# Attention, Fourier mixing and feed-forward in one kernel: the folded third token chunk contracted over all 128 rows in place of 97, 33 and 96

## The chip, the core and the metric

The kernel runs on one core of a Trainium2 chip. The metric is the device time of one execution in microseconds (us). Five engines work beside each other: TensorE (PE in the profile, with its weight loads as PEld), VectorE (DVE), ScalarE (ACT), GpSimd (POOL) and SyncE (SP, which issues the DMAs here). Before the change, three runs gave a median of 1114.37 us (1114.26 to 1114.49).

## The reference

Inputs are q, k, v of shape (8, 8, 576, 64), that is 8 batches, 8 heads, 576 tokens and 64 channels per head, and two weight matrices of 512 x 2048 and 2048 x 512.

```python
# attention, window of 128 tokens, with a slope of its own for each head
scores = scale * q @ k.T ; scores + bias inside the window, -1e9 outside
attn = softmax(scores) ; x = attn @ v          # heads side by side: (8, 576, 512)
# mixing
u = x + real(fft(fft(x, axis=tokens), axis=channels))
un = (u - mean) / sqrt(var + 1e-6)
out = u + relu(un @ w_ch1) @ w_ch2
```

The change lies in the Fourier step over the tokens.

## The kernel before, in words

**The whole.** The 8 batches are worked through in a pipeline. While one batch is in attention, the batch before it is in the Fourier step and the one before that in the feed-forward network. Each piece of work is a small Python function that is put in a queue with a due time (`put`, `after`); the queue is emptied in order of due time while the program is built, and this sets the order of the instructions on each engine. Nothing reorders the matmuls later: TensorE takes them as they come, so Fourier matmuls stand between score matmuls (`scores`, L382), value matmuls (`values`, L444 to L451) and the feed-forward matmuls (`ffn`, L720 and L734).

**Precision.** Most products are made of float16 halves: a number is the sum of a high and a low float16, and a product is high by high, low by high and high by low, added up in PSUM. In batches 0 and 1 the attention runs in float32.

**The Fourier step of a batch** is the function `fourier`. The 576 tokens are folded by symmetry (token t with token 576 - t), so that 289 token frequencies are computed from 289 folded tokens, in three chunks of 128, 128 and 33 (the array `X` and its third tile `X2`). The channels are folded too, into four groups `g` of 128 channels: groups 0 and 1 need the cosine table, groups 2 and 3 the sine table.

- `fold_a` to `fold_d` (L508 to L566) make the folded chunks. Chunks 0 and 1 give a high tile `fh` and a low tile `fl` of 128 rows each. The third chunk has only 33 rows for the cosine and 32 for the sine. Its halves are stacked in one tile of 128 partitions, called `stack` (and `stack1` for one extra channel): for the cosine groups the high half in rows 0 to 32 and the low half in rows 64 to 96; for the sine groups the high half in rows 0 to 31 and again in rows 32 to 63, the low half in rows 64 to 95. `stack` and `stack1` are set to zero once at the start (L122, L123).
- `rows(g)` (L568) multiplies: for each group, six matmuls of 128 rows for chunks 0 and 1, and then the third chunk. For the cosine groups that is one matmul over the first 97 rows of `stack` (high by high and low by high at once) and one over its first 33 rows (high by low); for the sine groups one over 96 rows does all three. Each matmul moves 289 columns of the table `tab1_sb` past 128 stationary columns and has a line of the profile, L576. The result goes through `rows_hi` on ScalarE (L580) and `rows_lo` on VectorE (L584) into float16 halves.
- `middle` (L586, matmuls at L593) does the same for one extra channel. Here the table is stationary and the moving operand is one column. It runs over three parts `j` of the frequencies (128, 128 and 33 wide), each with six matmuls of 128 rows, one of 97 and one of 33.
- `cols` (L604, matmuls at L610) is the Fourier step over the channels, `cols_out` and `cols_add` bring it back into `X`, and `norm` prepares the feed-forward input `uT`, which a transposing DMA writes.

In the third chunk of the table, `tables` sets everything to zero and then fills in (L826 to L828): entry 0 holds the cosine's high half in rows 0 to 32 and again in rows 64 to 96, entry 1 its low half in rows 0 to 32, entry 2 the sine's high, low and high halves in rows 0 to 31, 32 to 63 and 64 to 95.

Of the kernel before, what the change touches and what calls it, by code (L numbers as in the profile page):

```python
# [55 lines left out]
def begin_of(p):  # L56
    return 6 * PACE[0] * p if p < 4 else T1 + 6 * (p - 4)
# [6 lines left out]
def forward_of(b):  # L64
    return transform_of(b) + (START - DFT if b else 11 * PACE[1])
# [11 lines left out]
def attn_fft_ffn_kernel(  # L77
# [31 lines left out]
    tab1_sb = const.tile([128, 4, 3, NS], F16, name="tab1_sb")  # L109
# [11 lines left out]
    stack1 = const.tile([128, 1], F16, name="stack1")  # L121
# [369 lines left out]
    def bank(b):  # L491
        if b == 0:
            p = next(spare)
            return p.tile([128, 512], F32, name="fp" if p is ps_f else "pd")
        return ps_d.tile([128, 512], F32, name="pd")

    def fourier(b, t0):
# [70 lines left out]
        def rows(g):  # L568
            zp = st["zp", g] = bank(b)
            o = 0 if g < 2 else 2  # L570
            prods = [(st["in", c][l][:, g], tab1_sb[:, o + t, c]) for c in range(2) for l, t in ((0, 0), (1, 0), (0, 1))]
            rest = stack[:, 128 * g:128 * g + 128]
            for t, m in ((0, 97), (1, 33)) if g < 2 else ((2, 96), ):
                prods.append((rest[:m], tab1_sb[:m, t, 2]))
            for x, (l, r) in enumerate(prods):
                T.matmul(zp[:, :NS], l, r, start=(x == 0), stop=(x == len(prods) - 1))  # L576

# [8 lines left out]
        def middle():  # L586
            gps = st["gps"] = bank(b)
            for j, (j0, mj) in enumerate(SCH):
                prods = [(tab1_sb[:, t, c, j0:j0 + mj], st["in", c][2][:, x:x + 1])
                         for c in range(2) for t, x in ((0, 0), (0, 1), (1, 0))]  # L590
                prods += [(tab1_sb[:m, t, 2, j0:j0 + mj], stack1[:m]) for t, m in ((0, 97), (1, 33))]
                for x, (l, r) in enumerate(prods):
                    T.matmul(gps[:mj, j:j + 1], l, r, start=(x == 0), stop=(x == len(prods) - 1))  # L593

# [54 lines left out]
        t = t0 + f * 2.6  # L649
        for g in range(4):  # L650
            put(t, rows, g)
            put(t + f * 0.3, rows_hi, g)
            put(t + f * 0.5, rows_lo, g)
            t += f * 0.75
        put(t, middle)
        put(t + f * 0.2, middle_out)
        t += f * 0.55
# [86 lines left out]
    for p in range(4 * B):  # L744
        b, j = divmod(p, 4)
        t, f = begin_of(p), 1 if b else PACE[0]
# [23 lines left out]
    for b in range(B):  # L770
        t = begin_of(4 * b)
# [4 lines left out]
        t = forward_of(b)  # L776
# [119 lines left out]
```

## Time and profile before

| | before |
|---|---|
| median of 3 runs | 1114.37 us |
| time of the profiled execution | 1109.96 us |
| its span | 1108.2 us |
| around the span | 1.8 us |
| TensorE busy (matmuls) | 1061.6 us, 96% of the span |
| TensorE weight loads busy | 740.5 us, 67% |
| VectorE busy | 722.2 us, 65% |
| ScalarE busy | 584.8 us, 53% |
| mean granted TensorE clock | 0.961 |
| Fourier matmuls with the third chunk, L576 | 48 (16 of 97 rows, 16 of 33, 16 of 96) |
| the same, L593 | 48 (24 of 97 rows, 24 of 33) |

Matmuls overlap, and a matmul's duration in the profile is from its start to its modelled end. What a matmul costs TensorE is read from the start of one to the start of the next. In a row of the timeline the first number is the start in us from the span's start, the second the time that the row's instructions cover, then come engine, line, operation, out<-in, the array part that a matmul takes (rows*columns), the moving operand (rows x columns, type) and the number of instructions (x). An idle time before it and what ended it stand in brackets. The profiled execution's time is 4.4 us below the median of the runs; differences are taken between executions of one kind.

### The profile page before, as it was taken

How to read it: one execution, taken by the hardware profiler on the slowest of the kernel's cores; microseconds unless marked ns; L12 is line 12 of the kernel's file. 1: busy time of each engine (PE TensorE's matmuls, PEld its weight loads, DVE VectorE, ACT ScalarE, POOL GpSimd, SP SyncE). 2: the span in 40 equal slices, each digit the busy share in tenths (PEclk: the TensorE clock that was granted, in tenths of full speed). 3: DMA queues.
4: the chain of work that ended last, by engine and by line, in shares of the span. 5: the costliest groups of instructions: out<-in, count | busy, mean ns of one | idle time of the engine just before them, and what ended most of it. 6: DMA issues, size and time to landing. Idle time of an engine off the chain costs nothing.

```text
span 1108.2 us, 23754 instructions
## 1 busy us (share of the span) xinstructions
PE 1061.6 (96%) x9188; PEld 740.5 (67%) x9188; DVE 722.2 (65%) x2105; ACT 584.8 (53%) x1388; POOL 21.4 (2%) x61
## 2 busy tenths in 40 slices
PE   6989979989797999999999999999999999999998
PEld 5777767565564767667667677585857577767665
DVE  6989378837884576787868485969685755362111
ACT  5867589757855655456635464456535441241000
POOL 0000000000100000000000000001000000010000
PEclk9989569999899999999999999999999999999999
DMA  9951246667765544343643145334532240020000
GB/s 368 313 194 57 59 131 179 175 169 178 160 169 164 139 102 105 75 98 68 139 84 80 41 106 104 86 82 102 121 77 48 49 90 1 20 54 14 20 10 20
DMA packets 191506, 117.81 MB, mean 106 GB/s; under 512 B 154400, under 2 KB 164128, under 8 KB 191392
## 3 DMA queue, kind: packets, MB, share of 16 engines
q1 hardware_dynamic: 190816, 114.84, 40.6%
q8 instruction: 72, 1.18, 0.4%
q10 hardware_dynamic: 576, 1.45, 0.3%
q14 instruction: 42, 0.34, 0.1%
HBM read 70.63 MB, written 9.44 MB: 72 GB/s over the span
## 4 chain that ended last, share of the span: by engine, by line
PE 78%; DVE 8%; DMA 7%; ACT 4%; issue 2%; SPq 0%; POOL 0%; ACTq 0%; DVEq 0%
PE fp L720 31%; PE fp L734 27%; PE sp L382 6%; PE pv L444 3%; PE pd L576 3%; DMA wall<-q_dram 2%; DMA wall<-v_dram 2%; PE fp L303 2%; PE sp L425 1%; PE pd L610 1%; DMA uT<-un 1%; ACT wall L261 1%; DMA pt<-P 1%; PE pv L449 1%; DVE P L394 1%
## 5 line engine op out<-in xcount | busy, mean ns | idle before, releaser
L734 PE MATMUL fp<-wall,hbuf 128*128 128x512 f16 x1728 | 392.1, 379 | 0.3 <-DVE hbuf L162 0.3
L720 PEld LDWEIGHTS <-wall 128*128 128x128 f16 x3840 | 339.6, 99 | 63.6 <-issue 15.2
L720 PE MATMUL fp<-uT,wall 128*128 128x256 f16 x3072 | 366.1, 276 | 15.8 <-DVE hbuf L162 9.5
L734 PEld LDWEIGHTS <-hbuf 128*128 128x128 f16 x1728 | 161.8, 98 | 182.2 <-issue 3.5
L162 ACT ACTIVATE P<-P,nb 128x256 f32<-128x256 f32 x320 | 142.0, 479 | 107.1 <-DVE nb L394 107.0
L725 ACT ACTIVATE hbuf<-fp 128x512 f16<-128x512 f32 x144 | 84.9, 590 | 186.6 <-PE fp L720 186.6
L162 DVE SCALAR_TENSOR_TENSOR hbuf<-fp,hbuf 128x512 f16<-128x512 f32 x144 | 98.8, 687 | 127.5 <-ACT hbuf L725 127.1
L394 DVE CUSTOM_DVE_ANT_0 P<-sp,rg,nsl 128x256 f32<-128x256 f32 x240 | 97.5, 450 | 53.1 <-PE sp L382 48.5
L162 DVE SCALAR_TENSOR_TENSOR P<-P 128x256 f16<-128x256 f32 x240 | 88.7, 390 | 23.4 <-ACT P L407 21.9
L382 PE MATMUL sp<-kk,qq 64*128 64x256 f16 (+5 forms) x880 | 97.1, 297 | 6.5 <-DMA kk<-k_dram 5.3
L407 ACT ACTIVATE P<-P 128x256 f16<-128x256 f32 x240 | 85.2, 383 | 2.0 <-DMA pt<-P 1.7
L261 ACT ACTIVATE wall<-wall 128x512 f32<-128x512 f32 (+2 forms) x90 | 54.6, 607 | 50.2 <-DMA wall<-v_dram 23.2
L449 PE MATMUL pv<-vhs,pt 128*128 128x65 f16 x432 | 55.9, 196 | 4.6 <-DVE nmr L687 4.3
L450 PE MATMUL pv<-vl,pt 128*128 128x64 f16 x432 | 56.5, 194 | 0.0
L451 PE MATMUL pv<-vhs,pt 128*128 128x65 f16 x432 | 56.4, 195 | 0.0
L162 DVE SCALAR_TENSOR_TENSOR X<-fp,misc,X 128x512 f32<-128x512 f32 x32 | 23.8, 745 | 43.6 <-PE fp L734 43.6
L444 PE MATMUL pv<-vr,pt 128*128 128x65 f32 x288 | 47.7, 326 | 4.0 <-issue 2.3
L449 PEld LDWEIGHTS <-pt 128*128 128x128 f16 x432 | 41.3, 98 | 14.7 <-issue 7.7
L444 PEld LDWEIGHTS pv<-vr,pt 128*128 128x128 f32 x288 | 45.1, 242 | 7.6 <-issue 4.9
L382 PEld LDWEIGHTS <-qq 64*128 64x128 f16 (+1 forms) x720 | 31.3, 99 | 24.4 <-issue 20.6
L720 PE MATMUL fp<-wall,wall 128*128 128x128 f16 x768 | 45.4, 219 | 0.1
L450 PEld LDWEIGHTS <-pt 128*128 128x128 f16 x432 | 41.0, 99 | 6.4
(159 smaller groups left out, 1201.8 us busy)
## 6 DMA issues: line engine op xcount, KB each, us to landing
qr<-q_dram SPq DMA_DIRECT2D x32, 304.0 KB, 3.1
hbuf<-w_dram SPq DMA_DIRECT2D x16, 512.0 KB, 6.7
out_dram<-X SPq DMA_DIRECT2D x32, 256.0 KB, 2.4
wall<-v_dram SPq DMA_DIRECT2D x30, 256.0 KB, 2.9
vr<-v_dram SPq DMA_DIRECT2D x24, 320.0 KB, 3.4
kr<-k_dram SPq DMA_DIRECT2D x24, 289.0 KB, 3.3
wall<-q_dram SPq DMA_DIRECT2D x24, 256.0 KB, 2.9
wall<-k_dram SPq DMA_DIRECT2D x24, 256.0 KB, 2.8
```

Source lines behind the costliest of these rows:

```text
L162: put(now[0] + dt, lambda: f(*a, **kw))
L261: A.activation(t, t, AF.Square, accum_out=box["mx"][:, i, c:c + 1])
L382: T.matmul(sp[e][:m, col:col + n], qq[h, c0:c0 + m], keys(kk[h], ti), start=(x == 0), stop=(x == len(prods) - 1))
L394: V.tensor_tensor_reduce(pt[:m, 0:n], sp[e][:m, col:col + n], tab[:m, pc:pc + n], mul, 3.0e38, ALU.add, ALU.min, nb[:m, ti:ti + 1])
L407: A.activation(hi, P32, AF.Copy, scale=2.0 ** 14)
L444: T.matmul(pv[:, ti], pt[:, col:col + 128], ops[p][2][:, e, vc], start=first, stop=last)
L449: T.matmul(pv[:, ti], ph, vh[:, e, vc], start=first, stop=False)
L450: T.matmul(pv[:, ti, 0:D], ph, vl[:, e, vc], start=False, stop=False)
L451: T.matmul(pv[:, ti], pl, vh[:, e, vc], start=False, stop=last)
L720: T.matmul(fp[:, i * n:(i + 1) * n], w1_ap(e, c, f0 + i), uT[:, j, c, 0:n], start=(c == 0 and p == 0), stop=(c == 3 and p == 2))
L725: A.activation(ht[:, 0], fp, AF.Relu)
L734: T.matmul(op, hh[f][:, a, i * 128:(i + 1) * 128], w2_ap(e, f), start=(f == 0 and p == 0), stop=(f == 15 and p == 2))
```

## The change

The slices are dropped. `rows` and `middle` multiply over all 128 rows of `stack` and `stack1` and of the third chunk of the table. Between and behind the halves either the stacked tile or the table is zero (or both), so the sums stay the same. No instruction is added or removed, and the order of the instructions on all five engines, their waits included, is the same row by row in the built programs.

```diff
@@ rows(g)
             rest = stack[:, 128 * g:128 * g + 128]
-            for t, m in ((0, 97), (1, 33)) if g < 2 else ((2, 96), ):
-                prods.append((rest[:m], tab1_sb[:m, t, 2]))
+            for t in (0, 1) if g < 2 else (2, ):
+                prods.append((rest, tab1_sb[:, t, 2]))
             for x, (l, r) in enumerate(prods):
                 T.matmul(zp[:, :NS], l, r, start=(x == 0), stop=(x == len(prods) - 1))
@@ middle()
                 prods = [(tab1_sb[:, t, c, j0:j0 + mj], st["in", c][2][:, x:x + 1])
                          for c in range(2) for t, x in ((0, 0), (0, 1), (1, 0))]
-                prods += [(tab1_sb[:m, t, 2, j0:j0 + mj], stack1[:m]) for t, m in ((0, 97), (1, 33))]
+                prods += [(tab1_sb[:, t, 2, j0:j0 + mj], stack1) for t in (0, 1)]
                 for x, (l, r) in enumerate(prods):
                     T.matmul(gps[:mj, j:j + 1], l, r, start=(x == 0), stop=(x == len(prods) - 1))
```

## The prediction

> **What bounds the kernel now.** I read the page first (busy times and the chain of waits), then the table of stages, then TensorE's waits, and last the timeline around the Fourier matmuls.
>
> ```profile
> span 1108.2 us, 23754 instructions
> PE 1061.6 (96%) x9188; PEld 740.5 (67%) x9188; DVE 722.2 (65%) x2105; ACT 584.8 (53%) x1388; POOL 21.4 (2%) x61
> PE 78%; DVE 8%; DMA 7%; ACT 4%; issue 2%; SPq 0%; POOL 0%; ACTq 0%; DVEq 0%
> ```
>
> TensorE carries 78% of the chain that ends last. The rest must be placed in time, since time saved on TensorE ahead of a wait for another engine may be lost there. The table of stages has, after the stretch, busy us of PE, PEld, DVE, ACT and POOL, then the granted clock and the DMA share:
>
> ```profile
> 104.00:144.00 40.00, 39.30 (x192) 29.14 (x191) 19.25 (x59) 22.58 (x58) 0.17 (x2) 0.53 0.22 64
> 144.00:170.00 26.00, 19.91 (x110) 15.93 (x107) 20.50 (x67) 22.67 (x57) 1.70 (x6) 0.68 0.58 145
> 355.00:362.00 7.00, 3.03 (x16) 2.14 (x16) 3.05 (x7) 5.92 (x17) 0.00 (x0) 0.51 0.52 140
> 385.00:968.00 583.00, 581.38 (x5510) 398.22 (x5509) 409.54 (x1201) 288.88 (x688) 11.24 (x27) 1.00 0.36 80
> ```
>
> From 385 to 968 us TensorE is busy for 581.38 of 583 us at full clock: nothing else sets the pace there, and five of the eight Fourier steps (batches 3 to 7) lie in it. Before 385 us there are gaps, and stretches at about half clock. TensorE's waits (in all, times, longest) put names to them:
>
> ```profile
> PE fp L720 <- DVE hbuf L162: 9.5, 6, 6.6
> PE pv L449 <- DVE nmr L687: 4.3, 1, 4.3
> ```
>
> **The change part by part.** No instruction is added, removed or moved, and none waits for anything new. What can change is only the time of each matmul over the third chunk. First, a cosine group of batch 4 in the timeline, then a sine group of the same batch:
>
> ```profile
> 602.79 0.30 PE L576 MATMUL pd<-tab_sb,fh 128*128 128x289 f16 x1
> ...
> 603.42 0.29 PE L576 MATMUL pd<-tab_sb,fh 128*128 128x289 f16 x1
> 603.54 0.51 PE L576 MATMUL pd<-tab_sb,stack 97*128 97x289 f16 x2
> 603.99 2.69 PE L720 MATMUL fp<-uT,wall 128*128 128x256 f16 x23
> ```
>
> ```profile
> 616.14 0.29 PE L576 MATMUL pd<-tab_sb,fh 128*128 128x289 f16 x1
> 616.26 0.29 PE L576 MATMUL pd<-tab_sb,stack 96*128 96x289 f16 x1
> 616.39 1.58 PE L720 MATMUL fp<-uT,wall 128*128 128x256 f16 x13
> ```
>
> From start to start a matmul of 128 rows takes 603.54 - 603.42 = 0.12 us; the six from 602.79 to 603.54 take 0.75, or 0.125 each. The one of 96 rows takes 616.39 - 616.26 = 0.13, the same. But the pair of 97 and 33 rows takes 603.99 - 603.54 = 0.45, where two plain ones take 0.25. So 0.20 us is lost around the 33 rows, and none around 96 or 97. I read it as two stops of the array of about 0.10 us, one going into the 33 rows and one coming out. Whatever the mechanism, a product of 128 rows with neighbours of 128 rows is what the first six are, so I price the changed pair at 0.25 us. The sine groups change from 0.13 to 0.125: nothing.
>
> A cosine group gains 0.20 us and there are two in a batch: **0.40 us per batch**.
>
> [...]
>
> Now the middle step of the same batch:
>
> ```profile
> 621.96 0.29 PE L593 MATMUL pd<-a,tab_sb 128*128 128x1 f16 x6
> 622.11 0.27 PE L593 MATMUL pd<-stack,tab_sb 97*128 97x1 f16 x2
> 622.32 0.30 PE L593 MATMUL pd<-a,tab_sb 128*128 128x1 f16 x6
> 622.48 0.27 PE L593 MATMUL pd<-stack,tab_sb 97*128 97x1 f16 x2
> 622.68 0.30 PE L593 MATMUL pd<-a,tab_sb 128*33 128x1 f16 x6
> 622.85 0.27 PE L593 MATMUL pd<-stack,tab_sb 97*33 97x1 f16 x2
> 623.05 1.47 PE L734 MATMUL fp<-wall,hbuf 128*128 128x512 f16 x6
> ```
>
> Six matmuls with one column take 0.15 us (621.96 to 622.11), or 0.025 each, so a pair would take 0.05. The three pairs take 0.21, 0.20 and 0.20: 0.15 too much each, in two stops of some 0.075. That is six stops in the step. But the third part is only 33 columns wide, and other matmuls of that width show that this is a stop too:
>
> ```profile
> 519.32 0.38 PE L734 MATMUL fp<-wall,hbuf 128*128 128x512 f16 x1
> 519.63 0.23 PE L610 MATMUL pd<-tab_sb,zh 128*33 128x129 f16 x1
> 520.26 0.22 PE L610 MATMUL pd<-tab_sb,zh 128*33 128x127 f16 x1
> 520.41 0.82 PE L734 MATMUL fp<-wall,hbuf 128*128 128x512 f16 x3
> ```
>
> These two rows of 33 columns are the first and the last of twelve. The last takes 520.41 - 520.26 = 0.15 us up to the full-width matmul, where the eleven before it take (520.26 - 519.63) / 11 = 0.06 each: again a stop of about 0.09. So after the change two of the six stops stay, one into the narrow part and one out of it. Four go, worth 4 x 0.075 = **0.30 us per batch**. If the narrow part stopped nothing, all six would go (0.45); if the four stops left behind half their price, 0.15. I take 0.30.
>
> In batch 0 the clock is at half, and a stop there may cost more:
>
> ```profile
> 121.64 0.80 PE L576 MATMUL fp<-tab_sb,stack 97*128 97x289 f16 x2
> 122.38 0.42 PE L576 MATMUL pd<-tab_sb,fl 128*128 128x289 f16 x1
> 122.59 0.45 PE L576 MATMUL pd<-tab_sb,fh 128*128 128x289 f16 x1
> 122.83 0.80 PE L576 MATMUL pd<-tab_sb,stack 97*128 97x289 f16 x2
> 123.57 0.42 PE L576 MATMUL fp<-tab_sb,fl 128*128 128x289 f16 x1
> ```
>
> The pairs take 0.74 each, two plain ones 2 x 0.24 (122.59 to 122.83): 0.26 lost, 0.52 for both groups, with the middle step about 0.8 us.
>
> The counts are as the program has them:
>
> ```profile
> L576 PEld LDWEIGHTS <-stack x48: 92/98/152, 121.4 to 962.4; 97*128 97x128 f16 x16, 33*128 33x128 f16 x16, 96*128 96x128 f16 x16
> ```
>
> Sixteen groups of 33 rows are two in each of eight batches. TensorE's time saved is thus 7 x 0.70 + 0.8 = **5.7 us**. The weight loads of `stack` last 98 ns at the median whatever their rows, so the wider ones cost nothing.
>
> How much of this reaches the end? Batches 3 to 7, 5 x 0.70 = 3.5 us, lie in the stage where TensorE lost 1.6 of 583 us: all of it. In batch 2 the first cosine group stands just before TensorE's longest wait, so its 0.2 us only lengthens that wait; the other 0.5 us come after it, in a stretch of TensorE work: 0.5. For batch 1 one sees the same twice:
>
> ```profile
> 245.04 0.28 PE L576 MATMUL pd<-tab_sb,fh 128*128 128x289 f16 x1 [1.23 <-DVE zl L584]
> 358.97 1.44 PE L720 MATMUL fp<-uT,wall 128*128 128x256 f16 x6 [6.57 <-DVE hbuf L162]
> ```
>
> Its two cosine groups come before the wait that ends at 245.04, and the chain there runs through loads and ScalarE. Its middle step is on the chain, but the chain then goes over to VectorE and to the 4.3 us wait of L449, and from there through a row of loads to 358.97:
>
> ```profile
> 327.40 4.07 DMA wall<-k_dram
> 352.45 3.06 DMA wall<-q_dram
> ```
>
> These loads come one behind the other, each after ScalarE has read the slot. They start earlier if their first one does, and that hangs on VectorE and on SP's queue. For batches 0 and 1 (0.8 + 0.7) the bounds are therefore nothing and 1.5 us; I take half, 0.7. The sum is 3.5 + 0.5 + 0.7 = 4.7 us. Made against the profiled execution it gives 1109.96 - 4.7 = 1105.3; against the median of the runs, **1114.37 - 4.7 = 1109.7 us**.
>
> **The rivals.**
>
> *The early part keeps its time.* The load rows and VectorE set the pace up to 359 us, so nothing of batches 0 and 1 and little of 2 arrives: 3.5 us, 1110.9. For it speaks the 6.57 us wait, which a saving on TensorE alone can't shorten; against it, that the chain reaches these loads through work which TensorE feeds.
>
> *Everything arrives, or a little more.* 5.7 us, 1108.7. With it could come that the clock returns a step earlier in the stretch of 104 to 144 us, since TensorE stands still less there. Two us at half clock less are worth 1 us: 1107.7.
>
> *The rows don't matter.* The gap around the pair belongs to something else, to the operands or to the end of an accumulation, and stays. Then only the durations count:
>
> ```profile
> L576 PE MATMUL pd<-tab_sb,fh 128*128 128x289 f16 x116 | 27.8, 292 | 1.3 <-DVE zl L584 1.2
> L576 PE MATMUL pd<-tab_sb,stack 33*128 33x289 f16 x15 | 4.5, 303 | 0.0
> L576 PE MATMUL pd<-tab_sb,stack 97*128 97x289 f16 x15 | 4.5, 298 | 0.0
> ```
>
> 33 rows last 303 ns and 97 rows 298 against 292: 16 x 11 + 16 x 6 ns = 0.3 us, or 1114.1. Against it speaks that the 96-row matmul reads the same tiles, ends an accumulation and has no gap, and that L593 has the same gap with other operands. [...]
>
> *Slower through the clock.* Where TensorE arrives earlier at a wait that it can't shorten, it stands still longer, and the rows at 355 (0.51) and 144 (0.68) show that the granted clock falls around such waits. One more stretch like that of 144 to 170 us costs 26 x 0.32 = 8.3 us: 1114.4 - 4.7 + 8.3 = 1118.0. The point from which it decides: 9.4 us more at half clock eat the whole gain. For it speaks that three of the quoted stretches ahead of 385 us, 73 us in all, have a clock of 0.51 to 0.68 by their rows; against it, that the waits grow by 0.2 to 0.8 us where they last from 1 to 6.6 us already.
>
> **How the numbers follow.** The forecast has 0.55, the early part keeping its time 0.20, everything arriving 0.12, the rows not mattering 0.08, slower through the clock 0.05. A difference under 0.2% (2.2 us) can't be told from no change here. The first three are all beyond it: faster 0.87, same 0.08, slower 0.05. The range goes from 1107.6 (everything, and a little from the clock) to 1112.0 (the steady stage alone, less a little more than 1 us that a worse order of loads may take in the early part); the last two cases lie outside it.
>
> **What would show it.** In the changed profile, the pair at L576 has to stand 0.25 us before the next matmul, in place of 0.45, and carry 128*128; the middle step has to fall from 1.09 us (621.96 to 623.05) to about 0.79, with two stops left at its 33-wide part. From the batch-3 Fourier step on, the same piece of work should come 0.7 us earlier per batch, 3.5 in all between 385 and 968 us. The wait at 358.97 should be longer by up to 0.2 us, and what lies before 385 us says whether batches 0 to 2 brought 0.5 or 2.2 us. The forecast is wrong if the gap of the pair stays, or if the granted clock's mean falls below 0.955 from 0.961.

## The result, and the profile after

The changed kernel takes 1097.55 us (median of 4 runs, 1096.36 to 1105.40) beside 1114.32 us before: ratio 0.9869, 95% interval 0.9822 to 0.9917. Two later measurements of it gave 0.9910 (0.9874 to 0.9945; 1101.48 beside 1111.91 us) and 0.9881 (0.9853 to 0.9910; 1100.71 beside 1114.34 us). It is faster, as forecast, but by 10 to 17 us where 4.7 were forecast, and the first median lies below the range of 1107.6 to 1112.0.

The page of the changed kernel's profiled execution, whose own time is 1096.36 us:

```profile
span 1094.6 us, 23754 instructions
PE 1045.4 (96%) x9188; PEld 732.2 (67%) x9188; DVE 722.2 (66%) x2105; ACT 584.7 (53%) x1388; POOL 21.3 (2%) x61
```

The stops went as forecast. The timeline of TensorE around the same cosine group and the same middle step of batch 4:

```profile
592.45 0.29 PE L576 MATMUL pd<-tab_sb,fh 128*128 128x289 f16 x1
592.57 0.41 PE L576 MATMUL pd<-tab_sb,stack 128*128 128x289 f16 x2
592.82 2.78 PE L720 MATMUL fp<-uT,wall 128*128 128x256 f16 x24
```

```profile
610.77 0.29 PE L593 MATMUL pd<-a,tab_sb 128*128 128x1 f16 x6
610.92 0.19 PE L593 MATMUL pd<-stack,tab_sb 128*128 128x1 f16 x2
610.98 0.29 PE L593 MATMUL pd<-a,tab_sb 128*128 128x1 f16 x6
611.13 0.19 PE L593 MATMUL pd<-stack,tab_sb 128*128 128x1 f16 x2
611.24 0.31 PE L593 MATMUL pd<-a,tab_sb 128*33 128x1 f16 x6
611.41 0.19 PE L593 MATMUL pd<-stack,tab_sb 128*33 128x1 f16 x2
611.53 1.47 PE L734 MATMUL fp<-wall,hbuf 128*128 128x512 f16 x6
```

The pair takes 592.82 - 592.57 = 0.25 us in place of 0.45. The middle step takes 0.76 in place of 1.09 (forecast: 0.79). The pairs of its first two parts now take 0.06 and 0.11, and the third 0.12: two stops are left, one into the 33-wide part and one out of it.

The rest of the gain is in the granted clock of batch 0. The table of stages of the kernel before and of the changed kernel (busy us of PE, PEld, DVE, ACT, POOL, then the clock) over the stretch in which the clock was at half:

```profile
105.80:119.00 13.20, 13.20 (x50) 9.85 (x48) 10.74 (x32) 8.37 (x16) 0.10 (x1) 0.50 0.08 25
119.00:143.40 24.40, 24.40 (x132) 18.24 (x131) 6.39 (x21) 11.81 (x37) 0.00 (x0) 0.50 0.29 86
```

```profile
105.80:119.00 13.20, 13.20 (x50) 9.88 (x48) 10.54 (x30) 8.15 (x16) 0.10 (x1) 0.50 0.07 19
119.00:143.40 24.40, 21.73 (x189) 16.76 (x187) 15.87 (x56) 21.15 (x67) 0.20 (x2) 0.99 0.43 125
```

Up to 119.0 us both do the same. Then the clock stays at half until 143.4 in the one and is at full in the other, which runs 189 matmuls in that time where 132 ran before. Some 11 us come from there. How they and the rest add up can be read from the last matmul of batch 0's step over the channels and from the first matmul of the middle step in batches 2 and 7, first of the kernel before, then of the changed one:

```profile
143.53 0.22 PE L610 MATMUL pd<-tab_sb,zh 128*33 128x127 f16 x1
384.34 0.29 PE L593 MATMUL pd<-a,tab_sb 128*128 128x1 f16 x6
965.79 0.29 PE L593 MATMUL pd<-a,tab_sb 128*128 128x1 f16 x6
```

```profile
132.16 0.22 PE L610 MATMUL pd<-tab_sb,zh 128*33 128x127 f16 x1
375.28 0.29 PE L593 MATMUL pd<-a,tab_sb 128*128 128x1 f16 x6
952.53 0.29 PE L593 MATMUL pd<-a,tab_sb 128*128 128x1 f16 x6
```

The changed kernel is ahead by 11.4, 9.1 and 13.3 us, and by 13.6 at the end. Of the lead out of batch 0 some 2 us are lost in waits up to batch 2 (TensorE's longest wait lasts 7.10 us in place of 6.57, where at most 0.2 more was forecast), and the rest arrives. From batch 2 to batch 7 it gains 4.2 us; the forecast's terms for that piece are 0.30 + 4 x 0.70 + 0.40 = 3.5, and 0.6 more comes from the wait at 544.78, 0.87 us before and 0.3 after:

```profile
544.78 1.47 PE L720 MATMUL fp<-uT,wall 128*128 128x256 f16 x12 [0.87 <-DVE X L162]
```

```profile
PE fp L720 <- DVE X L162: 0.3, 1, 0.3
```

One thing in this execution speaks against the change as the cause of the clock's return. Its first matmul that differs is the pair at 120.48 us, after the return:

```profile
120.36 0.29 PE L576 MATMUL fp<-tab_sb,fh 128*128 128x289 f16 x1
120.48 0.41 PE L576 MATMUL fp<-tab_sb,stack 128*128 128x289 f16 x2
120.72 0.29 PE L576 MATMUL pd<-tab_sb,fl 128*128 128x289 f16 x1
```

In this one execution, then, the change can't have caused the return, and the 11 us that came with it are luck. So the experiments had to find out whether the early return belongs to the change at all.

### The profile page after: what moved, and what is told of

It reads as the page before. It is cut to its first block, busy times and chain, and to the rows that moved or that the text cites. A ratio compares the mean times of both kernels' runs of the same rounds, so it can differ in the third digit from the quotient of the medians.

```text
span 1094.6 us, 23754 instructions
## 1 busy us (share of the span) xinstructions
PE 1045.4 (96%) x9188; PEld 732.2 (67%) x9188; DVE 722.2 (66%) x2105; ACT 584.7 (53%) x1388; POOL 21.3 (2%) x61
## 4 chain that ended last, share of the span: by engine, by line
PE 73%; DVE 9%; DMA 8%; ACT 6%; issue 2%; SPq 1%; ACTq 0%; DVEq 0%
PE fp L720 29%; PE fp L734 27%; PE sp L382 5%; PE pd L576 2%; DMA wall<-q_dram 2%; ACT wall L261 2%; PE pv L444 2%; DMA wall<-k_dram 2%; DMA wall<-v_dram 1%; PE pd L610 1%; ACT P L162 1%; DVE P L394 1%; DMA pt<-P 1%; PE pv L449 1%; DVE wall L194 1%
## 5 line engine op out<-in xcount | busy, mean ns | idle before, releaser
L444 PE MATMUL pv<-vr,pt 128*128 128x65 f32 x288 | 43.9, 308 | 3.1 <-issue 2.4
L444 PEld LDWEIGHTS pv<-vr,pt 128*128 128x128 f32 x288 | 41.4, 224 | 6.7 <-issue 3.4
```

Of the source, the lines that this page charges most:

```text
L444: T.matmul(pv[:, ti], pt[:, col:col + 128], ops[p][2][:, e, vc], start=first, stop=last)
```

## The experiments

**How the runs are read.** Each run comes with its mean granted clock. In the profiled executions the clock comes back early in batch 0 (by 127 us) where the mean is 0.964 or more, and at 141 to 144 us where it is 0.963 or less; one kernel whose order of instructions came out otherwise is left out of this. A run of 0.964 or more is therefore counted as an early return below; the bound was chosen from these profiles. It is not sharp: three runs of the kernel before are counted as early with times of 1109 to 1113 us, and three of the 65-row kernel with 1104.83 to 1105.49 us, where its late runs begin at 1105.54.

| kernel | rows of the cosine pair / sine | stops in the group step | early returns | median us, beside before |
|---|---|---|---|---|
| before | 97, 33 / 96 | yes | 8 of 81 | 1111.69 to 1114.34 |
| changed (3 times) | 128, 128 / 128 | no | 14 of 16 | 1097.55 to 1101.48 |
| group step only | 128, 128 / 128 | no | 6 of 6 | 1101.56, 1111.69 |
| batch 0 only | 128, 128 / 128 in batch 0 | no in batch 0 | 9 of 12 | 1104.76, 1111.69 |
| all but batch 0 | as before in batch 0 | yes in batch 0 | 1 of 12 | 1108.56, 1111.69 |
| middle step only | 97, 33 / 96 | yes | 3 of 12 | 1109.85, 1111.69 |
| 65 rows (twice) | 97, 65 / 96 | no | 6 of 17 | 1105.97, 1111.91; 1106.26, 1114.34 |
| 128 and 64 rows | 128, 64 / 128 | yes | 2 of 12 | 1112.72, 1112.38 |

**Which part of the change, and which batch.** Four kernels carry parts of the change; the order of the instructions is the same in all of them.

```diff
 # batch 0 only (and "b > 0" for all but batch 0), in rows(g); middle() likewise
-            for t, m in ((0, 97), (1, 33)) if g < 2 else ((2, 96), ):
+            for t, m in zip((0, 1) if g < 2 else (2, ), (128, 128) if b == 0 else (97, 33) if g < 2 else (96, )):
 # group step only: the change's edit of rows(g), middle() as before
 # middle step only: the change's edit of middle(), rows(g) as before
```

Batch 0 only:

> All 128 rows in batch 0 only; batches 1 to 7 as before. Theory A (the denser Fourier work of batch 0 is what lets the granted clock come back after 120 us instead of 143 us): 11 to 12 us less than before in nearly every run, mean clock about 0.97. Theory B (in the profile of the change the clock came back at 119.0 us, ahead of the first changed matmul at 120.5 us, so it hangs on where the clock's steps happen to lie, not on the change): 0.8 us less than before at equal clock, and early and late returns mixed here as they would be in the kernel before.

All but batch 0:

> All 128 rows in batches 1 to 7, batch 0 as before. Theory A: the clock comes back at 143 us as before (mean clock about 0.96) and only the stops of seven batches go: 4 to 5 us less than before. Theory B: the stops go too, 4 to 5 us at equal clock, and where the clock returns early 11 us more, as often as in the changed kernel.

The group step only:

> All 128 rows in the step over the four groups, 97 and 33 rows in the middle step. Stops: 8 batches x 0.40 us, some 3 us less than before at equal clock. Theory A: with the early return of the clock 12 to 15 us less in nearly every run, since the group step is what makes 120 to 124 us denser. Theory B: 3 us less, and the early return by chance.

The middle step only:

> All 128 rows in the middle step, 97, 33 and 96 rows in the group step. Four stops of 0.075 us in each batch go: 2.4 us less than before at equal clock. Theory A: the clock does not return early, since the group step of batch 0 at 120 to 124 us is as before: 2 to 2.5 us less, clock 0.96. Theory B: 2 to 2.5 us less, and the early return by chance.

Measured: ratios 0.9947 (0.9923 to 0.9971), 0.9958 (0.9935 to 0.9981), 0.9903 (0.9882 to 0.9923) and 0.9967 (0.9936 to 0.9999). In medians that is 6.9, 3.1, 10.1 and 1.8 us less, in each case under what theory A had given. Where the group step of batch 0 has all 128 rows, the early return comes in 15 of 18 runs; where it is as before, in 4 of 24. Theory B in its strict form, that the change has nothing to do with it, falls. Its lesser half stands: the return is a matter of chance, and the change moves the odds. The profiles of the first and the third kernel show the place. The table of stages, batch 0 only and then group step only:

```profile
103.80:124.30 20.50, 20.21 (x70) 13.71 (x70) 13.73 (x38) 12.57 (x26) 0.10 (x1) 0.50 0.12 35
124.30:143.40 19.10, 18.08 (x168) 14.51 (x166) 11.91 (x42) 16.22 (x54) 0.20 (x2) 1.00 0.48 143
```

```profile
103.60:124.10 20.50, 20.16 (x69) 13.70 (x70) 13.76 (x40) 12.63 (x26) 0.10 (x1) 0.50 0.13 34
124.10:143.40 19.30, 18.51 (x168) 14.77 (x166) 11.85 (x42) 16.29 (x54) 0.20 (x2) 1.00 0.48 142
```

Here the clock returns at 124, right behind the denser group step at 120 to 124 us. The two rows of batch 0 at half clock are 20.50 us long, and the kernel before had 37.5 (6 and 11 times 3.41 us): a difference of 17 us at half speed, so 8 to 9 us of work. All but batch 0 gained 3 us in its median (forecast 4 to 5), with the clock of the kernel before.

**The changed kernel once more**, on two other chips, for the spread:

> The changed kernel once more, for the spread of its runs. Theory A (denser Fourier work in batch 0 makes an early return of the granted clock likely): nearly all runs with a mean clock near 0.97, about 1096 to 1101 us, beside 1110 to 1112 for the kernel before. Theory B (the early return is chance and has nothing to do with the change): as many late returns as in the kernel before, with times around 1106.

> The changed kernel, on the same chip as the next one: the early return of the clock in most runs (9 of 10 so far were below 1105.5 us), late ones near 1107.

Ten of twelve runs have the early return, 1095.72 to 1101.94 us. The two others took 1107.48 and 1108.35 us beside medians of 1111.91 and 1114.34 us: 4.4 and 6.0 us less. Both happen to be profiled executions, and beside the profiled execution of the kernel before (1109.96 us) they are only 2.5 and 1.6 us less. So with a late return the change is worth some 2 to 6 us here, which two runs don't settle more closely. The first one's table of stages, and its middle steps of batches 2 and 7:

```profile
105.00:119.00 14.00, 14.00 (x53) 10.37 (x50) 11.23 (x33) 8.72 (x18) 0.10 (x1) 0.50 0.10 26
119.00:142.50 23.50, 23.50 (x129) 18.11 (x128) 6.13 (x20) 11.66 (x35) 0.00 (x0) 0.50 0.30 91
```

```profile
386.00 0.29 PE L593 MATMUL pd<-a,tab_sb 128*128 128x1 f16 x6
963.60 0.29 PE L593 MATMUL pd<-a,tab_sb 128*128 128x1 f16 x6
```

It is 1.7 us behind the kernel before at batch 2 and 2.2 ahead at batch 7: 3.9 us gained in the steady stage (forecast 3.5). The second is 2.9 behind at batch 2 (387.25) and 1.3 ahead at batch 7 (964.50), 4.2 gained. Both are 0.7 us ahead at the last matmul of batch 0's step over the channels (142.81 and 142.84 against 143.53; 0.8 forecast), and up to batch 2 they lose that and more. The early part differs by a few us from run to run in all these kernels, the kernel before too.

**Stops or rows?** The change does two things to the group step: it takes the stops away, and it lets more rows of the array work. Two kernels do one without the other. With 65 rows in place of 33 there are no stops but hardly more rows; with 128, 64 and 128 there are nearly all the rows but all the stops.

```diff
 # 65 rows, in rows(g); middle() likewise
-            for t, m in ((0, 97), (1, 33)) if g < 2 else ((2, 96), ):
+            for t, m in ((0, 97), (1, 65)) if g < 2 else ((2, 96), ):
 # 128 and 64 rows
+            for t, m in ((0, 128), (1, 64)) if g < 2 else ((2, 128), ):
```

> 97 rows as before, and 65 in place of 33 (rows 33 to 64 meet zeros in the table). Theory stops (the array stops where matmuls over at most 64 rows stand beside wider ones): no stops at the group step, two left in the middle step, so like the changed kernel within 0.3 us of TensorE time, and its early return of the clock too: 1096 to 1102 us. Rival (what helps is that all operands have the same full shape): the stops stay, 0.2 us around each 65-row matmul, and the time is that of the kernel before.

> 97 and 65 rows, 96 for the sine: no stops, but fewer rows than the changed kernel. If the removed stops alone bring the early return of the clock: as often as in the changed kernel beside it. If the clock counts rows times columns: its group step fills fewer rows (1188 against 1408 rows over its eleven matmuls from 121 us on), so the early return comes clearly less often, in a fifth to a half of the runs; the late ones near 1106.5 us, which is the gain of the stops alone, 4 to 5.5 us below the kernel before.

> 128 rows in place of 97 and 96, and 64 in place of 33 (the rows between meet zeros): nearly the work of the changed kernel by rows, but with all stops of the kernel before. Theory stops: at equal clock the time of the kernel before, within 1 us, with 0.45 us for the pair in the group step; if the threshold is not at 64 rows, the stops go and it is 4 to 5 us less. Theory C (rows count for the clock): the early return in more runs than in the kernel before, half or more. Theory C2 (stops hold the clock down): as seldom as in the kernel before, one run in eight.

The timeline around a cosine group, with 65 rows and then with 128 and 64:

```profile
597.20 0.41 PE L576 MATMUL pd<-tab_sb,stack 97*128 97x289 f16 x2
597.45 0.19 PE L449 MATMUL pv<-vhs,pt 128*128 128x65 f16 x1
```

```profile
604.24 0.51 PE L576 MATMUL pd<-tab_sb,stack 128*128 128x289 f16 x2
604.69 1.48 PE L720 MATMUL fp<-uT,wall 128*128 128x256 f16 x12
```

The pair takes 0.25 us with 65 rows and 0.45 with 64. The bound of the stop lies between 64 and 65 rows, and the rival, that the full shape matters, falls. In time, 65 rows give 0.9946 (0.9915 to 0.9978) and 0.9935 (0.9912 to 0.9957), or 6 and 8 us less, with the early return in 6 of 17 runs; the expectation to see it as often as in the changed kernel failed. 128 and 64 rows give 0.9989 (0.9964 to 1.0014), no gain, and the early return in 2 of 12. Neither part alone brings the early return of the changed kernel; both together bring it in 14 of 16 runs. If the clock counted rows alone, 128 and 64 rows should have brought it in half of the runs or more; the 2 of 12 are what was expected if stops hold the clock down.

**The array by itself.** To see what the clock counts, a kernel of its own leaves out the whole computation and runs eleven streams of 120 matmuls with 8 to 9 us of idle time between them. It ran once.

```diff
+    def stream(*kinds):                     # rows r, width c, in turn
+        for i in range(120):
+            r, c = kinds[i % len(kinds)]
+            T.matmul(pt[:c, 0:289], w[:r, :c], x[:r], start=True, stop=True)
```

> A kernel of its own, not the reference's computation: TensorE idles for about 25 us, then runs 120 matmuls of 289 columns without a break, eleven times over, with other rows each time: 128, 97, 65, 64, 33, then in turn 128/33, 128/65, 128/97, then 128 columns wide in turn with 33 wide, then 128 rows of which 96 hold zeros, then 128 again. Theory stops: from start to start 0.12 us at full clock for every single kind, and about 0.10 us more for each change only in 128/33 and in 128/33 wide, none in 128/65 and 128/97. Theory C (the clock counts rows times columns): the clock returns after one or two steps of 3.4 us with 128 rows, later or not at all with 65, 64 and 33 rows. Theory C2 (it counts only whether the array is moving columns): it returns as early with 33 rows as with 128, and late or never only where stops stand. Zero rows: the same as 128 if the rows taken count, as 33 if the data counts.

The table of stages of that kernel (busy us of PE, PEld, ACT, POOL, then the clock). Its rows are, in order: 97 rows in two pieces, 65 rows, 64, 33, 128 and 33 in turn, 128 and 65 in turn in two pieces, 128 and 33 columns wide in turn, and 128 rows with zeros in 96 of them in two pieces:

```profile
31.70:37.50 5.80, 5.80 (x25) 3.62 (x25) 5.55 (x9) 0.00 (x0) 0.50 0.00 1
37.50:49.10 11.60, 11.60 (x96) 9.20 (x95) 11.03 (x19) 0.00 (x0) 1.00 0.01 1
58.70:87.40 28.70, 28.66 (x119) 17.87 (x119) 18.25 (x29) 0.00 (x0) 0.50 0.00 1
96.00:124.70 28.70, 28.70 (x119) 17.41 (x119) 18.24 (x29) 0.00 (x0) 0.50 0.00 1
133.30:162.00 28.70, 28.70 (x120) 17.37 (x119) 18.21 (x29) 0.00 (x0) 0.50 0.00 1
170.50:212.50 42.00, 41.98 (x119) 12.09 (x118) 18.26 (x29) 0.00 (x0) 0.50 0.00 0
221.10:225.20 4.10, 4.10 (x18) 2.55 (x18) 3.91 (x7) 0.00 (x0) 0.50 0.02 4
225.20:238.00 12.80, 12.80 (x104) 9.95 (x103) 12.20 (x20) 0.00 (x0) 1.00 0.00 0
275.20:317.70 42.50, 42.46 (x120) 12.49 (x119) 18.25 (x29) 0.00 (x0) 0.50 0.00 0
326.20:331.00 4.80, 4.80 (x20) 2.98 (x21) 4.58 (x8) 0.00 (x0) 0.50 0.01 3
331.00:343.20 12.20, 12.20 (x100) 9.69 (x99) 11.63 (x19) 0.00 (x0) 1.00 0.00 0
```

This shows that rows in use count for the clock. A stream of 97 rows gets the full clock after 5.8 us, 128 and 65 in turn after 4.1. A stream of 65, 64 or 33 rows never gets it in its 28.7 us, although TensorE is busy from one end to the other. That refutes C2, that only moving columns count: the rows used count with them. With 51% of the rows in use (65 of 128) the clock stays at half, with 75 to 76% (97, or 128 and 65 in turn) it comes back; in such streams the bound lies between. Rows that meet zeros in the moving operand count as rows in use (4.8 us). Whether the width in columns counts as rows do isn't shown, since 33 columns ran only in turn with 128, with the stops that this brings.

It also prices the stops. At half clock 128 and 33 rows in turn take 42.0 / 119 = 0.35 us a matmul, where a single kind takes 28.7 / 119 = 0.24: 0.11 us for each change. The changes between 128 and 33 columns wide cost the same (42.5 / 120 = 0.35). At full clock 128 and 65 in turn take 12.8 / 104 = 0.12: no stop.

The group step of batch 0 is in keeping with this, if what counts is the rows in use over time, so that a stop lowers the count too. In the kernel before, its eleven matmuls from 121.19 to 124.41 us use 1124 rows, added up over the matmuls (2 x (128 + 128 + 97 + 33) + 128 + 128 + 96) in 3.22 us, where 3.22 / 0.241 = 13.4 matmuls of 128 rows would fit: 66% of the array. With 128, 64 and 128 rows it is 1280 rows in the same time, 75%. With 65 rows it is 1188 rows, and without stops they last eleven times 0.241 us: 84%, but for 2.65 us only. The changed kernel has 100% in 2.65 us. What stands beside it, from 119.18 us up to it and again from 124.41 us in the kernel before, is float32 work, whose weight in the count I can't read from these runs, so how far each of these is from the bound stays an estimate.

The stretches at half clock in batch 0 last multiples of 3.41 us in these profiles (20.5 is 6 of them, 37.5 is 11, and the 13.6 of the profiled changed kernel, from 105.4 to 119.0, are 4). The later ones of the two kernels do so too: 153.6 to 170.7 us (5), 225.3 to 228.7 (1), 286.7 to 297.0 (3) and 355.0 to 361.8 (2) in the kernel before, 142.9 to 160.0 (5), 276.1 to 286.3 (3) and 344.3 to 354.6 (3) in the changed one. So the time from the fall of the clock on is counted here in steps of 3.41 us. The group step begins 15.4 us after the fall in the kernel before (105.8 and 121.19) and 17.2 us after it with the group step only (103.6 and 120.77), so the same matmuls lie in other places of the steps from one execution to the next. That this is what makes the return a matter of chance is an estimate of mine from these places; no run shows it by itself.

For the group step the profiles are in keeping with it. Counted so from where the clock fell, the eleven matmuls lie whole within one step in batch 0 only (120.92 to 123.69 us, step 120.85 to 124.26) and in group step only (120.77 to 123.54, step 120.70 to 124.11), and the clock returns at the end of that step. In the two late executions of the changed kernel the clock fell at 105.0 and 105.6 us, so a step ends inside the group step, at 122.1 and 122.7, and the clock did not return there or at the next step's end. With 65 rows in its second measurement the group step lies whole in a step too (121.09 to 123.86, step 120.79 to 124.21), but the clock stays at half beyond it:

```profile
103.80:124.30 20.50, 20.03 (x69) 13.64 (x70) 13.89 (x40) 12.66 (x26) 0.10 (x1) 0.50 0.12 34
124.30:141.30 17.00, 17.00 (x105) 14.39 (x105) 4.04 (x14) 7.55 (x25) 0.00 (x0) 0.50 0.36 102
```

The same holds for 128 and 64 rows (120.51 to 123.73, step 120.41 to 123.83), where the clock stays at half until 144.3. So at a like place of the steps full rows without stops brought the clock back, and either part alone did not, in one execution of each. It isn't the whole rule: the version with filled waits, further down, has its group step cut by a step's end at 122.1 and the clock returned at 125.5 all the same. Why the profiled changed kernel returned at 119.0, ahead of its first changed matmul, stays open too: in two late executions (middle step only, and the changed kernel's second) a step ends within 0.1 and 0.3 us of the same place among the same matmuls, and the clock did not return.

**Work added to bring the clock back.** The kernel before, with useless matmuls behind each group of batch 0, and a control with the same number of matmuls of one column.

```diff
+            for _ in range(4 if b == 0 else 0):
+                T.matmul(zp[:, NS:512], stack[:, 128 * g:128 * g + 128], tab1_sb[:, 0, 0, 0:223], start=True, stop=True)
 # the control: zp[:, NS:NS + 1] and tab1_sb[:, 0, 0, 0:1]
```

> The kernel before, with its stops, plus four useless matmuls of 223 columns behind each of the four groups of batch 0 (into unused columns of the same bank; the output is the same). They cost 16 x 0.19 = 3 us at half clock, 1.5 at full. Theory A in its activity form (the clock comes back when a step of 3.4 us holds enough matmul work): the clock returns at about 124 to 130 us in place of 143, so 4 to 7 us less than before, although work was added. Rival A2 (the stops themselves hold the clock down): it returns at 143 us or later, 2 to 3 us more than before. Theory B: the same 2 to 3 us more, with early returns as seldom as before.

> Control for the kernel with useless matmuls: the same sixteen instructions, but with one column each, so that they add 16 x 0.025 to 0.05 us of array time. Theory A in its activity form and rival A2: late return as before, within 1 us of before. If merely the changed order of instructions moved the clock, this kernel would show the early return as well.

It decided nothing by its time: 1134.48 us, ratio 1.0212 (1.0168 to 1.0256), far above all three expectations. With the sixteen matmuls the instructions came out in another order when the program was built (some 600 of TensorE's 9188 other matmuls stand elsewhere), and new waits came with that, as its waits of TensorE show (before, neither was among them; its L612 is L610 of the others):

```profile
PE pv L449 <- DMA pt<-P: 7.5, 2, 6.0
PE pd L612 <- ACT ab L624: 5.8, 1, 5.8
```

In its profile the clock did come back early, at 127.2 us. That agrees with theory A, but it is one execution. Its six runs lie at two levels, 1129.19 to 1131.63 and 1137.33 to 1139.38 us, three in each, and the profiled one is in the lower; that the other two there returned early as well isn't shown. The control took 1108.08 us, 0.9969 (0.9938 to 1.0001), with 2 early returns in 10. It is no control for the order: only 16 of TensorE's matmuls stand elsewhere in it. So the early return at 127.2 may come from the added work or from the new order.

**Two versions that might beat the change.** One fills the wait at 103 us with useless matmuls; the other also makes the 33-wide parts 128 wide, by taking columns behind the table's piece into partitions that nobody reads.

```diff
 # first version, in turn(), ahead of the transposes
+        for _ in range(3 if p == 4 else 0):
+            T.matmul(tp[:, 0:256], tab1_sb[:, 0, 0, 0:128], tab1_sb[:, 0, 0, 0:256], start=True, stop=True)
 # second version, in middle(); in cols() likewise, on tiles of 384 columns with zeros behind
-                    T.matmul(gps[:mj, j:j + 1], l, r, start=(x == 0), stop=(x == len(prods) - 1))
+                    T.matmul(gps[:, j:j + 1], l, r, start=(x == 0), stop=(x == len(prods) - 1))
```

> A version that may beat the changed kernel: the same, plus three useless matmuls of 256 columns ahead of each set of transposes of the first head pair of batch 1, where TensorE waits 1.8 us for ScalarE at 103 us and the clock falls to half at 105 us (they write a bank that the transposes overwrite; the output is the same). 18 x 0.11 = 2 us of matmuls, about half of it in the wait. If the clock falls at 105 us because of that wait: no fall, and 5 to 8 us less than the changed kernel. If the order of the instructions that the planner makes of it costs more (it changes on every engine): slower than the changed kernel by several us.

> A version that may beat the changed kernel: the same, and the 33-wide parts of the middle step and of the step over the channels are made 128 wide as well (columns behind the table's piece, or zeros, into partitions that nobody reads; the output is the same). Theory stops: in each batch the middle step loses its last two stops (0.15 us) and the third part of the step over the channels two of 0.09 us, 0.33 us a batch or 2.6 us in all below the changed kernel at equal clock. The planner makes another order of it, which by the runs so far can cost or bring several us.

The first took 1101.54 us, ratio 0.9900 (0.9877 to 0.9922), no better than the change. The clock fell at 105.0 us all the same. The second took 1099.54 us, 0.9873 (0.9847 to 0.9898), beside the changed kernel's 0.9881 (0.9853 to 0.9910) on the same chip: not to be told apart. Its last stops did go:

```profile
618.86 0.29 PE L596 MATMUL pd<-a,tab_sb 128*128 128x1 f16 x6
619.01 0.19 PE L596 MATMUL pd<-stack,tab_sb 128*128 128x1 f16 x2
619.06 0.59 PE L737 MATMUL fp<-wall,hbuf 128*128 128x512 f16 x2
```

The pair takes 0.05 us, and the whole middle step 619.06 - 618.45 = 0.61 in place of 0.76.

## Why the prediction was right and wrong

- **The price of the stops was right.** 0.20 us was forecast for a cosine pair and 0.20 was measured; 0.30 for the middle step, and 1.09 - 0.76 = 0.33 was measured. The choice that two of six stops stay was right, and the second version shows that they belong to the 33-wide part.
- **The steady stage was right.** From batch 2 to batch 7 the profiles show 4.2 us, and 3.9 and 4.2 in the two executions with a late return, for 3.5 forecast.
- **The rival that rows don't matter** falls: the pair went from 0.45 to 0.25 us, and 65 rows do the same.
- **At the clock of the kernel before, the forecast of 4.7 us is in keeping with the runs**, not more: 4.4 and 6.0 us in the two runs of the changed kernel with a late return, beside the medians before, and 2.5 and 1.6 beside the profiled execution before. The late runs of the 65-row kernel, without the same stops, are 5.0 to 6.4 us below the median before in its first measurement (1105.54 to 1106.87 beside 1111.91).
- **The step that failed** is the clock in batch 0. The sum of the forecast, 3.5 + 0.5 + 0.7, leaves the granted clock as it was and has no term for it. It stands only in the rival that everything arrives: "the clock returns a step earlier in the stretch of 104 to 144 us, since TensorE stands still less there. Two us at half clock less are worth 1 us". The mechanism was named, but its size was a guess that no row gave, and its chance was set at a part of 0.12. What the runs show in its place: the changed kernel has the early return in 14 of 16 runs (8 of 81 before), and in the profiles with an early return of the changed kernel and its parts the stretch at half clock is 17 to 24 us shorter than before, worth 8 to 12 us. The row of 104 to 144 us (clock 0.53 over 40 us) should have set the upper end: at 0.47 below full, a clock at full all through is worth up to 19 us.
- **Its reason was half of it.** TensorE standing still less, without more rows, brought the early return in 6 of 17 runs (65 rows). That 128 rows count for more than 97 and 33 was not in the prediction; it takes both (14 of 16). And in the profiled execution the return came before any changed matmul, which no reason of the prediction covers.
- **That half of the gain in batches 0 and 1 arrives** was too low for a lead of this size: of 11.4 us out of batch 0, 9.1 are there at batch 2's middle step, behind the load rows. The rival that the early part keeps its time falls for it. For the stops of these batches alone it isn't settled, since the early part differs by a few us from run to run.
- **The rival of a slower clock** didn't occur: no run of the changed kernel had a mean clock below 0.961.
- **The row of weight loads was read too closely.** Its 98 ns are the median of three shapes together; by shape the means are 105 (97 rows), 104 (96) and 93 ns (33). The forecast doesn't hang on it: the changed pair takes 0.25 us.

## What to carry to other kernels

Read the cost of a matmul from start to start, and look for a change of array part between neighbours: 33 or 64 rows, or 33 columns wide, beside full ones cost some 0.1 us going in and again coming out, and in these runs filling them up to full with zeros or unread columns took it away (for the rows, 65 were enough). Where a profile shows a long stretch at half clock with TensorE busy throughout, ask what share of the array's rows the matmuls fill, since streams of 65 rows and fewer kept the clock down for as long as they ran, 28.7 us. And where one run in ten already shows the other state of the clock, take many runs and count.

## What the runs showed of the hardware that was not expected

- Rows in use count for the clock: streams of 33, 64 and 65 rows stayed at half clock for 28.7 us without a break, 97 rows had the full clock after 5.8 us, and 128 rows of which 96 met zeros had it after 4.8.
- A change of width (128 to 33 columns and back) costs as much as a change of rows, 0.11 us at half clock.
- The bound lies between 64 and 65 rows: 0.45 us for a pair with 64, 0.25 with 65.
- A program's time can have two levels by when the clock returns: the kernel before took 1100.87 to 1104.07 us in 5 of 81 runs and 1109.28 to 1117.25 in the others, and the change mostly moves runs from the upper level to the lower.
